# Attention values of a pair in two blocks, with a new chunk order, in a fused attention and expert kernel

## The chip, the cores and the metric

The kernel runs on one core of one Trainium2 chip. The metric is the device time of the whole kernel in microseconds. TensorE (PE; PEld is its weight load), VectorE (DVE), ScalarE (ACT), GpSimd (POOL) and SyncE (SP, the queue of plain DMAs) each run their own instructions in order and wait for one another by semaphores.

## The reference

```python
# attention: batch 8, heads 8, sequence 576, head size 64
scores = q @ k^T / 8
cum = cumsum(maximum(s, 0))
scores = where(j > i, -1e9, scores + minimum(cum[j] - cum[i], 0))
attn = exp(scores - max); attn = attn / (sum(attn) + 1e-9)
out = attn @ v                          # reshaped to x: 4608 rows of 512 (8 heads x 64)
# mixture of experts: 8 experts, 512 -> 1024 -> 512
logits = x @ w_gate + modality_bias[modality_id]
e = argmax(logits); gate = softmax(logits)[e]
y = gate * (relu(x @ w1[e]) @ w2[e])    # one expert a row
```

## The kernel before

The work has two stages. Attention runs over 32 pairs: a pair is one head in two batches (0 and 1 of `ab`), and eight pairs, one for each head, finish the rows of two batches. Then those rows are routed: their expert is chosen and they are scattered by expert into lists in DRAM. The expert stage (class `Moe`) reads the lists in blocks of 256 rows and streams the weights of the block's expert; its first weights are loaded during the last pairs.

**A pair.** The 576 query rows of each batch are cut into four chunks of 128 and a rest of 64; the two rests share one chunk. So a pair has nine chunks: 0 to 3 for batch 0, 4 to 7 for batch 1, and 8 for both rests. Chunk i (below 8) sees `128 * (i % 4 + 1)` keys, chunk 8 all 576. `ORDER` lists the chunks as they are worked. `run` (L334) has one step for each chunk of each pair, nine steps a pair, and each step issues in this order:

- `score` of the chunk. TensorE multiplies q and k in two matmuls (L236, L237; chunk 8 has eight, L250, L251): operands are split into a rounded high part and a low part. QH and KA hold high parts (KA's upper half k's low part), QL and KB the low part of q against the high part of k, and the bias rows. VectorE adds the mask and takes the extreme of each row (L239, L253), ScalarE takes the exponential and its row sum (L259). Four PSUM banks (`sp`) hold scores.
- in the steps named by `setup` and at fixed places: constants, and the loads of a later pair (`load`).
- one piece of `prep` of the next pair: POOL copies q and k to QH, KA and KB (`high`, L178) and subtracts for the low parts of k (L196, twice) and of q for batch 1 (L198). The low part of q for batch 0 (L192) is VectorE's, in the third piece. Each pair alternates between two sets of QH, QL, KA, KB.
- one piece of `tail` of the pair before.
- `trans` of the chunk that was scored three steps ago (`LAG`): TensorE transposes it in blocks of 128 into one of two PSUM banks (`pt`), and ScalarE (VectorE for chunk 8) copies it to PT (L272, L284). Chunk 8 takes two such banks, four blocks and one block. PT has three buffers for the batches of two pairs.
- one piece of routing, if a group of eight pairs is done (`Route.group`; L491 to L536: reductions and comparisons on VectorE, ten small matmuls, and nine scatters by POOL, one in four steps).

**The tail** starts when the last chunk in `ORDER` is transposed, and one step later (`TD`) issues the values: for both batches five matmuls over the keys into one bank `om` (queries 128 to 575, L307) and one into the bank `ox` (queries 0 to 127, L305). ScalarE copies the result to oT (L313, L314), VectorE the two rests (L317), side by side as a block diagonal. The next two steps multiply oT with pw, a matrix that is identity and w_gate side by side for each batch (L203), so that rows come out with their expert logits behind them (72 columns a row and head): first for chunks 0 and 1 of both batches, then for 2 and 3 and the rests, these in two matmuls of 72 columns that accumulate. VectorE scales the result by the reciprocal row sums (L311, L312) into x (L329, L331). These, the small matmuls of routing and oT's first part share the one bank `ox`.

**Order.** The program names which instruction an engine may take only after which (`issue_after`): the values come after all TensorE work issued ahead of them, and what is issued later stays behind them (`self.wall`). `self.hold[0]` is the newest mask and extreme on VectorE. Between these points a scheduler lays the instructions of each engine in an order of its own, guided by the order of issue.

Of the kernel before, what the change touches and what calls it, by code (L numbers as in the profile page):

```python
# [12 lines left out]
ALU = mybir.AluOpType  # L13
# [11 lines left out]
ORDER = (3, 7, 2, 1, 8, 6, 5, 0, 4)  # L25
# [6 lines left out]
class Attn:  # L32
# [3 lines left out]
    def __init__(self, ctx, tc, qkv, s, ident, consts):  # L36
# [15 lines left out]
        self.pw = c.tile([P, 8, 2 * XW], F32, name="pw")  # L52
        self.mk = c.tile([P, 800], F32, name="mk")
# [50 lines left out]
    def setup(self, wg):  # L104
        nc = self.nc
        wgv = wg.rearrange("(h d) e -> d h e", d=64)
        for ab in range(2):
            nc.sync.dma_start(self.pw[64 * ab:64 * ab + 64, :, XW * ab + 64:XW * ab + XW], wgv)

    def consts(self, t1):  # L110
# [29 lines left out]
        for ab in range(2):  # L140
            rows = slice(64 * ab, 64 * ab + 64)
            idv = self.ident[rows, 64 * ab:64 * ab + 64]
            nc.scalar.copy(self.pw[rows, :, XW * ab:XW * ab + 64], idv.unsqueeze(1).broadcast_to([64, 8, 64]))

# [23 lines left out]
    def prep(self, pi):  # L168
# [21 lines left out]
        for a in range(2):  # L190
            if a == 0:
                nc.vector.tensor_tensor(QL[lo, a, :KW], rq[lo, a], QHf[lo, a, :KW], ALU.subtract)  # L192
# [68 lines left out]
    def trans(self, st, i):  # L261
# [24 lines left out]
    def tail(self, st):  # L286
# [5 lines left out]
        o0 = self.ps2.tile([P, 512], F32, name="ox")  # L292
        om = self.ps2.tile([P, 448], F32, name="om")
# [3 lines left out]
        for j in (0, 1, 2, 3, 4, -1):  # L297
            q0 = max(P * j, P)
            for ab in range(2):
                r = slice(64 * ab, 64 * ab + 64)  # L300
                with ExitStack() as after:
                    for i in pe:
                        after.enter_context(self.tc.issue_after(i))
                    if j < 0:
                        m = nc.tensor.matmul(o0[r, :P], V[:, ab, 0, :], PT[ab][:, :P], start=True, stop=True)  # L305
                    else:
                        m = nc.tensor.matmul(om[r, q0 - P:], V[:, ab, j, :], PT[ab][:, PTS * j + q0 if j < 4 else PTW - 64:PTS * j + KW if j < 4 else PTW], start=j == 0, stop=j == 4)  # L307
                pe = [m.ins]
        self.wall = m.ins
        rs = self.sm.tile([P, 9], F32, name="rs")  # L310
        nc.vector.tensor_tensor(rs, st["sums"], self.eps, ALU.add)  # L311
        nc.vector.reciprocal(rs, rs)  # L312
        nc.scalar.copy(oT[:, :P], o0[:, :P])  # L313
        nc.scalar.copy(oT[:, P:512], om[:, :384])  # L314
        for ab in range(2):
            r = slice(64 * ab, 64 * ab + 64)
            nc.vector.tensor_copy(oT[r, 512 + 64 * ab:576 + 64 * ab], om[r, 384:])  # L317
        yield
        for g in range(2):
            xo = self.ps2.tile([P, 512], F32, name="ox")  # L320
            for u in range(2):
                c = 2 * g + u
                self.pw_(xo[:, 2 * XW * u:2 * XW * u + 2 * XW], oT[:, P * c:P * c + P], self.pw[:, h, :], start=True, stop=True)
            if g == 1:
                for ab in range(2):
                    self.pw_(xo[:, 4 * XW:5 * XW], oT[:, 512:], self.pw[:, h, XW * ab:XW * ab + XW], start=ab == 0, stop=ab == 1)
            src = xo[:, :4 * XW].rearrange("p (t d) -> p t d", t=4)
            rv = rs[:, 4 * g:4 * g + 4].unsqueeze(2).broadcast_to([P, 4, XW])
            nc.vector.tensor_tensor(x[g][:, :, :, h], src.rearrange("p t (d r) -> p t d r", r=2), rv.rearrange("p t (d r) -> p t d r", r=2), ALU.mult)  # L329
            if g == 1:  # L330
                nc.vector.tensor_scalar(x[2][:, 0, :, h], xo[:, 4 * XW:5 * XW].rearrange("p (d r) -> p d r", r=2), rs[:, 8:9], None, ALU.mult)  # L331
            yield

    def run(self, npair, newx, done, setup):  # L334
# [5 lines left out]
        prev, prepg, n = None, None, len(seq)  # L340
        for k in range(n + LAG + 9):
# [14 lines left out]
            nt = None  # L356
            if LAG <= k < n + LAG:
                p0, i0 = seq[k - LAG]
                if i0 == ORDER[-1]:
                    nt = sts[p0]  # L360
            if prev is not None:
                if next(prev, 0) == 0:
                    prev = None
                    if ps["pi"] % 8 == 7:
                        bg.append(done(ps["pi"] // 8, ps["x"]))
            if LAG <= k < n + LAG:
                with self.behind():
                    self.trans(sts[p0], i0)
            if nt is not None:
                prev, ps = self.tail(nt), nt  # L370
            if prev is None and k >= n + LAG:
                break
# [4 lines left out]
        assert prev is None  # L377
# [633 lines left out]
```

## Time and profile before

| what | us |
|---|---|
| three runs | 923.99, 926.44, 930.06 |
| median | 926.44 |
| profiled execution, its own time | 922.89 |
| its span, first to last instruction | 921.1 |
| first values block / last values block / first expert matmul group | 42.3 / 437.6 / 443.3 |

Of the span TensorE is busy 91%, VectorE 67%, POOL 63%, ScalarE 56%. The mean granted TensorE clock is 0.977 of full speed. A row in order of time has start, duration, engine, line, operation, tile written and tiles read, shapes, count, and in brackets the engine's idle time just before it with what ended it. Rows of groups have busy time, mean duration in ns, idle time and releaser. An f32 matmul shows as two records, and for the values the two batches run side by side in the two halves of the array's columns.

### The profile page before, as it was taken

Reading aid. Unit: us, or ns where it says so; the run is one execution under the profiler, and the core shown is the slowest. Engines: PE = TensorE matmul, PEld = TensorE weight load, DVE = VectorE, ACT = ScalarE, POOL = GpSimd, SP = SyncE. Lnnn points to the kernel's source line nnn. Section 1 sums busy time; section 2 is a strip of 40 time slices with the busy share of each in tenths; the row PEclk is TensorE's granted clock in tenths of the full one; section 3 lists DMA queues with packets and bytes.
Section 4 is the critical chain, followed back from the end, with each engine's and each line's share of the span. In section 5 each row is a group of like instructions: output and inputs, shape, how many; then the busy total and the mean of one; then the engine's idle time right before and its main releaser. Section 6 shows DMA issues by size and latency. Waiting matters only on the chain. (4 is left out here: it accounts for less than half of the span.)

```text
span 921.1 us, 16713 instructions
## 1 busy us (share of the span) xinstructions
PE 834.6 (91%) x5584; PEld 697.2 (76%) x5584; DVE 615.7 (67%) x1486; ACT 519.4 (56%) x1209; POOL 575.9 (63%) x478
## 2 busy tenths in 40 slices
PE   0799998999899898988879989999999999999984
PEld 0577776767677776755769879999999999999862
DVE  7487777657866587666657966666666556665681
ACT  3577776767677666757434445445444445444651
POOL 9676776887687876872266555555655556555760
PEclk9999999999999999989989989999999999999998
DMA  5654444454454545424758676666666666665940
GB/s 149 198 138 138 137 137 138 152 171 136 135 157 152 165 125 173 143 89 145 256 188 306 257 273 242 231 231 232 232 230 231 227 222 226 221 227 221 309 161 2
DMA packets 67562, 172.76 MB, mean 188 GB/s; under 512 B 12087, under 2 KB 12087, under 8 KB 67412
## 3 DMA queue, kind: packets, MB, share of 16 engines
q1 hardware_dynamic: 61620, 151.64, 48.8%
q0 software_dynamic: 5856, 20.06, 5.5%
q8 instruction: 44, 0.72, 0.3%
q14 instruction: 42, 0.34, 0.1%
HBM read 144.95 MB, written 26.80 MB: 186 GB/s over the span
## 5 line engine op out<-in xcount | busy, mean ns | idle before, releaser
L259 ACT ACTIVATE pe<-pe,mx 128x512 f32<-128x512 f32 (+3 forms) x256 | 144.1, 564 | 48.0 <-DVE mx L239 48.0
L272 ACT COPY PT<-pt 128x512 f32<-128x512 f32 (+3 forms) x256 | 106.5, 419 | 52.3 <-PE pt L269 49.5
L239 DVE CUSTOM_DVE_ANT_0 pe<-sp,mk 128x512 f32<-128x512 f32 (+3 forms) x256 | 117.3, 480 | 27.4 <-PE sp L237 24.0
L269 PE MATMUL pt<-ident,pe 128*128 128x128 f32 x640 | 119.2, 287 | 15.3 <-ACT PT L272 13.2
L825 ACT ACTIVATE hT<-hp 128x512 fp32r<-128x512 f32 x72 | 42.8, 595 | 158.7 <-PE hp L823 158.7
L809 POOL DMA_INDIRECT out<-ys,oi x36 | 39.9, 1110 | 141.7 <-DVE ys L808 55.7
L236 PE MATMUL sp<-KA,QH 128*128 128x256 f32 (+2 forms) x256 | 98.4, 392 | 20.1 <-DVE KA L196 16.0
L269 PEld LDWEIGHTS pt<-ident,pe 128*128 128x128 f32 x640 | 79.2, 146 | 42.5 <-ACT PT L272 29.8
L196 POOL TENSOR_TENSOR KA<-rawk,KA 64x576 fp32r<-64x576 f32 x63 | 93.8, 1506 | 20.3 <-DMA lists<-x,di 18.2
L237 PE MATMUL sp<-KB,QL 76*128 76x256 f32 (+2 forms) x256 | 85.2, 336 | 13.6 <-DMA QL<-oh 7.2
L823 PE MATMUL hp<-xT,wcb 128*128 128x256 f32 x648 | 90.1, 283 | 0.0
L307 PE MATMUL om<-PT,V 128*64 128x448 f32 (+3 forms) x640 | 89.6, 427 | 0.0
L826 DVE SCALAR_TENSOR_TENSOR hT<-hp,hT 128x512 fp32r<-128x512 f32 x72 | 49.2, 684 | 59.3 <-ACT hT L825 59.2
L823 PE MATMUL hp<-xT,wcc 128*128 128x256 f32 x528 | 77.4, 287 | 7.8 <-DVE hT L826 3.2
L823 PEld LDWEIGHTS hp<-xT,wcb 128*128 128x128 f32 x648 | 83.6, 189 | 0.6
L178 POOL TENSOR_SCALAR QH<-rawq 128x576 fp32r<-128x576 f32 x62 | 41.5, 671 | 64.0 <-issue 56.3
L802 PE MATMUL y<-wcb,hT 128*128 128x512 f32 x336 | 81.1, 398 | 0.0
L307 PEld LDWEIGHTS om<-PT,V 128*64 128x64 f32 x640 | 44.0, 139 | 46.8 <-issue 37.5
L823 PE MATMUL hp<-xT,wca 128*128 128x256 f32 x552 | 78.7, 285 | 0.4 <-ACT xT L788 0.3
L823 PEld LDWEIGHTS hp<-xT,wcc 128*128 128x128 f32 x528 | 70.8, 196 | 9.0 <-DVE hT L826 3.4
L802 PEld LDWEIGHTS y<-wcb,hT 128*128 128x128 f32 x336 | 62.8, 188 | 14.8
L823 PEld LDWEIGHTS hp<-xT,wca 128*128 128x128 f32 x552 | 72.3, 191 | 1.3 <-ACT xT L788 0.5
(270 smaller groups left out, 1946.7 us busy)
## 6 DMA issues: line engine op xcount, KB each, us to landing
wrbw<-in_w SPq DMA_DIRECT2D x104, 512.0 KB
wraw<-in_w SPq DMA_DIRECT2D x56, 512.0 KB
rawq<-in_qkv SPq DMA_DIRECT2D x32, 576.0 KB
rawk<-in_qkv SPq DMA_DIRECT2D x32, 576.0 KB
xg<-lists SPq DMA_DIRECT2D x18, 576.0 KB
V<-in_qkv SPq DMA_DIRECT2D x32, 320.0 KB
lists<-z SPq DMA_DIRECT2D x8, 576.0 KB
ekd<-ek SPq DMA_DIRECT2D x1, 1440.0 KB
```

The costliest lines, as they stand in the source:

```text
L196: self.last = (nc.vector if pi == 0 and a == 0 else nc.gpsimd).tensor_tensor(KA[up, a], rk[up, a], KAf[up, a], ALU.subtract).ins
L236: self.pe.append(nc.tensor.matmul(sp[:, :nn], QH[:, q0:q0 + P], KA[:, ab, :nn], start=True, stop=False).ins)
L237: self.pe.append(nc.tensor.matmul(sp[:, :nn], QL[:EXT, q0:q0 + P], KB[:EXT, ab, :nn], start=False, stop=True).ins)
L239: ins = nc.vector.tensor_tensor_reduce(out=t[:, :n], in0=sp[:, :n], in1=self.mk[:, 512 - n:512], scale=-0.125, scalar=3.0e38, op0=ALU.add, ...
L259: nc.scalar.activation(t[:, :n], t[:, :n], AF.Exp, bias=m, scale=-1.0, accum_out=st["sums"][:, o:o + 1])
L269: self.pe.append(nc.tensor.transpose(out=pt[:, P * j:P * j + P], in_=pe[:, P * j:P * j + P], identity=self.ident).ins)
L272: cp(w[:, :, v:v + P], pt[:, :P * (c + 1)].rearrange("p (j q) -> p j q", q=P))
L307: m = nc.tensor.matmul(om[r, q0 - P:], V[:, ab, j, :], PT[ab][:, PTS * j + q0 if j < 4 else PTW - 64:PTS * j + KW if j < 4 else PTW], star ...
L802: self.last[0] = nc.tensor.matmul(y[u], hT[:, a, f, P * u:P * u + P], W[4 + f // 2][:, c, 512 * (f % 2):512 * (f % 2) + 512], start=f == 0 ...
L823: nc.tensor.matmul(hp[:, u], W[k][:, a, f:f + P], xT[:, c, k], start=k == 0 and i == 0, stop=k == 3 and i == 2)
L825: nc.scalar.activation(hs, hp, AF.Relu)
L826: nc.vector.scalar_tensor_tensor(hT[:, 1, 2 * m:2 * m + 2], hp, 0.0, hs.bitcast(F32), ALU.max, ALU.subtract)
```

## The change

1. `ORDER` becomes 3, 7, 2, 6, 8, 1, 5, 0, 4: the chunks with the most keys first.
2. The tail is split in two. The large block (`g` = 1: queries 256 to 575, five matmuls for each batch) starts when chunk 8, fifth in the order, is transposed; the small one (`g` = 0: queries 0 to 255, two matmuls for each batch) when the last chunk is. Each has its own values, one copy to oT of 256 columns, one step with the packed matmuls, and its own reciprocal sums, placed behind the newest mask and extreme. So values of the large block come at the start of the next pair, those of the small one where all values stood before. Both use one bank `o`; `ox` is left to the packed matmuls and routing. Routing of a finished group starts one step earlier.
3. The fifth block of chunk 8's transpose goes to the free columns of the bank `o` instead of to a second `pt` bank.
4. The two packed matmuls of the rests become one, with a second matrix `pq` (identity and w_gate for both batches below each other), filled by two more copies and two more DMAs at the start. `s8` is made in place of `sr`.
5. The low part of q for batch 0 moves from the third piece of `prep` to the first, behind the newest mask and extreme.

```diff
-ORDER = (3, 7, 2, 1, 8, 6, 5, 0, 4)
+ORDER = (3, 7, 2, 6, 8, 1, 5, 0, 4)
...
+        self.pq = c.tile([P, 8, XW], F32, name="pq")
...
-            s8 = t1.tile([64, KW], F32, name="s8")
+            s8 = sr
...
+            nc.sync.dma_start(self.pq[64 * ab:64 * ab + 64, :, 64:], wgv)
...
+            nc.scalar.copy(self.pq[rows, :, :64], idv.unsqueeze(1).broadcast_to([64, 8, 64]))
...
+        with self.tc.issue_after(self.hold[0]) if self.hold[0] is not None else ExitStack():
+            nc.vector.tensor_tensor(QL[lo, 0, :KW], rq[lo, 0], QHf[lo, 0, :KW], ALU.subtract)
         yield
...
-            if a == 0:
-                nc.vector.tensor_tensor(QL[lo, a, :KW], rq[lo, a], QHf[lo, a, :KW], ALU.subtract)
...
-                pt = self.ps1.tile([P, 512], F32, name="pt")
+                if nj == 4:
+                    pt = self.ps1.tile([P, 512], F32, name="pt")
+                else:
+                    st["o"] = self.ps2.tile([P, 512], F32, name="o")
+                    pt = st["o"][:64, 384:]
...
-    def tail(self, st):
+    def tail(self, st, g):
...
+        q0, q1 = (256, KW) if g else (0, 256)
+        o = st["o"] if g else self.ps2.tile([P, 512], F32, name="o")
         oT = self.oT[st["pi"] % 2]
 
         pe, self.pe = self.pe, []
-        for j in (0, 1, 2, 3, 4, -1):
+        nj = 5 if g else 2
+        for j in range(nj):
+            f = max(P * j, q0)
...
+                    m = nc.tensor.matmul(o[r, f - q0:q1 - q0], V[:, ab, j, :], PT[ab][:, PTS * j + f if j < 4 else PTW - 64:PTS * j + q1 if j < 4 else PTW], start=j == 0, stop=j == nj - 1)
+            pe = [m.ins]
         self.wall = m.ins
...
+        nc.scalar.copy(oT[:, q0:q0 + 256], o[:, :256])
+        if g:
+            for ab in range(2):
+                r = slice(64 * ab, 64 * ab + 64)
+                nc.vector.tensor_copy(oT[r, 512 + 64 * ab:576 + 64 * ab], o[r, 256:320])
+        yield
+        n = 5 if g else 4
+        rs = self.sm.tile([P, 5], F32, name="rs")
+        with self.tc.issue_after(self.hold[0]):
+            nc.vector.tensor_tensor(rs[:, :n], st["sums"][:, 4 * g:4 * g + n], self.eps[:, :n], ALU.add)
+            nc.vector.reciprocal(rs[:, :n], rs[:, :n])
...
+        if g:
+            self.pw_(xo[:, 4 * XW:5 * XW], oT[:, 512:], self.pq[:, h, :], start=True, stop=True)
...
+                if i0 in (8, ORDER[-1]):
+                    g = int(i0 == 8)
+                    prev.append((self.tail(sts[p0], g), sts[p0], g))
```

More of the change, by code (lines that the diff above doesn't have):

```diff
@@ L311, in tail @@
[L311 to L317, printed above, removed]
-        yield
[L319 to L332, printed above, removed]
@@ new lines, in tail @@
+        n = 5 if g else 4
[3 more added lines that the diff above has]
+            nc.vector.reciprocal(rs[:, :n], rs[:, :n])
+        xo = self.ps2.tile([P, 512], F32, name="ox")
+        for u in range(2):
+            c = 2 * g + u
+            self.pw_(xo[:, 2 * XW * u:2 * XW * u + 2 * XW], oT[:, P * c:P * c + P], self.pw[:, h, :], start=True, stop=True)
@@ L355, in run @@
                     next(prepg, 0)
-            nt = None
+            if prev and next(prev[0][0], 0) == 0:
+                _, st, g = prev.pop(0)
+                if g == 0 and st["pi"] % 8 == 7:
+                    bg.append(done(st["pi"] // 8, st["x"]))
             if LAG <= k < n + LAG:
                 p0, i0 = seq[k - LAG]
[L359 to L366, printed above, removed]
                 with self.behind():
                     self.trans(sts[p0], i0)
-            if nt is not None:
-                prev, ps = self.tail(nt), nt
-            if prev is None and k >= n + LAG:
+                if i0 in (8, ORDER[-1]):
+                    g = int(i0 == 8)
+                    prev.append((self.tail(sts[p0], g), sts[p0], g))
+            if not prev and k >= n + LAG:
                 break
@@ L376, in run @@
                         bg.pop(0)
-        assert prev is None
+        assert not prev
         return bg
```

16 lines of the change are left out of this document (6 added, 10 removed).

## The prediction

> **What bounds the kernel now.** I read the page first, then the windows, then the order of time on TensorE, and only then the engines that release it.
>
> ```profile
> span 921.1 us, 16713 instructions
> ...
> PE 834.6 (91%) x5584; PEld 697.2 (76%) x5584; DVE 615.7 (67%) x1486; ACT 519.4 (56%) x1209; POOL 575.9 (63%) x478
> ...
> 500.00:921.00 421.00, 399.93 (x2517) 356.44 (x2515) 268.94 (x297) 194.03 (x242) 229.55 (x105) 0.98 0.60 219
> ```
>
> TensorE is busy 91% of the span. The last row (PE, PEld, DVE, ACT, POOL busy, granted clock, DMA share, GB/s) is the expert stage, which the diff does not touch: PE 399.93 of 421 us. So what attention gives up or wins should move the end by as much. Next, one pair in the attention stage, in order of time (start us, us, engine, line, tiles, count):
>
> ```profile
> 66.66 2.70 PE L307 MATMUL om<-PT,V 128*64 128x448 f32 x20
> ...
> 69.51 0.66 PE L269 MATMUL pt<-ident,pe 128*128 128x128 f32 x4
> ...
> 71.57 1.16 PE L203 MATMUL ox<-pw,oT 128*128 128x144 f32 x8
> ...
> 72.56 0.27 PE L269 MATMUL pt<-ident,pe 128*128 128x128 f32 x1
> ...
> 77.19 0.27 PE L269 MATMUL pt<-ident,pe 128*128 128x128 f32 x1
> 77.93 0.33 PE L269 MATMUL pt<-ident,pe 128*128 128x128 f32 x1 [0.46 <-ACT PT L272]
> ...
> 78.51 2.70 PE L307 MATMUL om<-PT,V 128*64 128x448 f32 x20
> ```
>
> From one values block (L307) to the next: 78.51 - 66.66 = 11.85 us, with a single wait in it, 0.46 us for ScalarE to empty a transpose bank. That is the undisturbed pair. Now the disturbed ones and the end:
>
> ```profile
> 137.50 2.70 PE L307 MATMUL om<-PT,V 128*64 128x448 f32 x20
> ...
> 143.70 0.76 PE L203 MATMUL ox<-pw,oT 128*128 128x144 f32 x4 [2.34 <-ACT oT L313]
> ...
> 153.37 2.70 PE L307 MATMUL om<-PT,V 128*64 128x448 f32 x20
> ...
> 188.95 2.70 PE L307 MATMUL om<-PT,V 128*64 128x448 f32 x20
> ...
> 198.67 0.50 PE L237 MATMUL sp<-KB,QL 76*128 76x512 f32 x1 [1.81 <-POOL QL L198]
> ...
> 203.74 2.70 PE L307 MATMUL om<-PT,V 128*64 128x448 f32 x20
> ```
>
> (a row of the windows, columns as in the expert stage's)
>
> ```profile
> 199.00:202.50 3.50, 3.50 (x19) 3.18 (x18) 2.98 (x10) 2.97 (x10) 3.50 (x6) 0.67 0.97 317
> ```
>
> (and the end, in order of time)
>
> ```profile
> 437.58 0.60 PE L307 MATMUL om<-PT,V 128*64 128x448 f32 x2
> ...
> 442.34 1.16 PE L203 MATMUL ox<-pw,oT 128*128 128x144 f32 x8 [0.55 <-DVE x L329]
> ...
> 443.33 1.04 PE L786 MATMUL tp<-ident,xg 128*128 128x128 f32 x8
> ```
>
> The interval after 137.50 is 15.87 us, 4.02 over the undisturbed; it holds the routing of the batch pair just finished, and recurs after the 16th and 24th pair. I call it the **routing pair**. The interval after 188.95 is 14.79 us, 2.94 over: 1.81 us of waiting for POOL's low part of q, then a granted clock of 0.67 in the next 3.5 us. It ends each stretch in which POOL scatters rows (three times); I call it the **scatter pair**. The expert stage starts at 443.33, directly behind the last packed matmuls. Three intervals before each scatter pair look undisturbed, but POOL falls behind in them. That leaves 14 intervals where only TensorE's own work and the 0.46 us count: eight before the first routing pair, and three in each of the two batches after it.
>
> **The change part by part.**
>
> *Fifth packed block.* One matmul for two: two of the eight records at 71.57 go. They take (72.56 - 71.57) / 8 = 0.124 us each, though two pairs of them have half the columns; so the weight loads set the pace, and a pair saves 0.25 us of TensorE.
>
> *Values in two blocks.* Columns for each head: 448 + 448 + 320 + 192 + 64 + 128 = 1600 before; 3 x 320 + 192 + 64 for the large block and 256 + 128 for the small one, 1600 again. Twelve matmuls a pair become fourteen, but the cost of a block is columns plus its ends. The rate, from two weight loads of 448-column matmuls (two heads at once):
>
> ```profile
> 204.17 0.14 PEld L307 LDWEIGHTS om<-PT,V 128*64 128x64 f32 x2 [0.23 <-issue]
> ...
> 204.54 0.14 PEld L307 LDWEIGHTS om<-PT,V 128*64 128x64 f32 x2 [0.23 <-issue]
> ```
>
> 0.37 us for 448 columns, twice per matmul: 1600 columns take 2.64 us, while 66.66 to 69.51 is 2.85. One end costs about 0.2 us, and a second block pays it again; between 0.1 and 0.35 (the gap in front of the block included) I take 0.25. So the packed saving is spent here: TensorE's work stays the same.
>
> *What the 0.46 us wait hangs on.* VectorE and ScalarE ahead of it:
>
> ```profile
> 73.56 1.01 DVE L284 COPY PT<-pt 128x256 f32<-128x256 f32 x4
> ...
> 76.40 1.16 DVE L192 TENSOR_TENSOR QL<-rawq,QH 64x576 fp32r<-64x576 f32 x1
> ...
> 78.21 0.65 DVE L311 TENSOR_TENSOR rs<-sums,eps 128x9 f32<-128x9 f32 x1
> ...
> 79.49 0.80 ACT L259 ACTIVATE pep<-pep,mx 128x576 f32<-128x576 f32 x1
> ...
> 73.11 0.67 POOL L178 TENSOR_SCALAR QH<-rawq 128x576 fp32r<-128x576 f32 x1 [3.36 <-issue]
> ...
> 77.04 3.17 POOL L196 TENSOR_TENSOR KA<-rawk,KA 64x576 fp32r<-64x576 f32 x2
> ```
>
> Before the values, three large chunks are scored in a row while TensorE has only small transposes; ScalarE's exponentials queue up, and L192 (1.16 us) holds VectorE among their reductions. Then the 2.85 us values block lets both go idle. With the large block after the first score of the next pair, some 2 us of TensorE work lie between the scores of chunks 3 and 7, and L192 now sits there: POOL starts QH at 73.11 and ends its first half at 73.78, ahead of the reduction of chunk 3, so L192 does not wait for POOL in an undisturbed pair. The 0.46 us should go. Without that cover it would cost VectorE its 1.16 us again.
>
> *What is late next.* (1) The large block needs the four copies of chunk 8 (1.01 us of VectorE, at 73.56), which were five steps early before. Between its transposes and the block now stand the scores of chunks 4 and 3 and two transposes; 77.19 - 72.56 = 4.63 us hold six scores and ten transposes, so these are about 1 us: no margin, 0 to 0.3 us. (2) The packed matmuls of the small block need ScalarE's copy, which queues behind the 0.80 us exponential of chunk 8; before, 2.85 us of values lay over it, now the small block, 384 columns x 2 x 0.37 / 448 = 0.63 us and its ends, about 0.9. Wait 0 to 0.5. I take 0.1 for both together, since TensorE can fill either with scores that are ready. Net for an undisturbed pair: 0.46 - 0.1 = 0.36 us, and 14 x 0.36 = **5 us**. ScalarE's copies to oT stay level (512 columns in two copies, before and after). (3) The sums for the reciprocal now go in two parts; the large block's add stands in the step behind that block, where VectorE has little room and POOL is in L196. The row at 78.21 is this add beside L196 as it is now, 0.65 us; I keep that row, which the reductions behind it can bear.
>
> The Trainium skill, page "SBUF — State Buffer", section "SBUF: two separate sides", says that a VectorE instruction with two SBUF inputs and a GpSimd instruction that reads SBUF take one shared port pair as an exclusive lock, and the loser waits out the other's whole instruction. By it the add could be held for a whole L196 instead of 0.65 us, and the sum below would be that of the second rival, a loss.
>
> *Scatter pairs and the three before each.* POOL sets the pace there:
>
> ```profile
> 193.02 2.79 POOL L196 TENSOR_TENSOR KA<-rawk,KA 64x576 fp32r<-64x576 f32 x2 [2.31 <-DMA lists<-x,di]
> ...
> 197.22 1.39 POOL L198 TENSOR_TENSOR QL<-rawq,QH 64x576 fp32r<-64x576 f32 x1
> ```
>
> A faster TensorE only waits longer for L198. Scatters start one step earlier, same number. **0 us**, between -2 and +2 for each of three; L192 ahead of a late POOL can hold VectorE, up to about 1 us, mostly under the large block.
>
> *Routing pairs.*
>
> ```profile
> 136.29 3.31 POOL L196 TENSOR_TENSOR KA<-rawk,KA 64x576 fp32r<-64x576 f32 x2
> ...
> 138.26 1.43 DVE L496 TENSOR_TENSOR lg<-lg,rmx 128x72 f32<-128x72 f32 x1
> ...
> 139.96 1.22 DVE L500 SCALAR_TENSOR_TENSOR oh<-lg,ew 128x72 f32<-128x72 f32 x1
> ...
> 142.14 0.23 DVE L503 TENSOR_TENSOR ohb<-oh,rmx 128x72 bf16<-128x72 f32 x1
> ...
> 74.49 0.27 DVE L239 CUSTOM_DVE_ANT_0 pe<-sp,mk 128x128 f32<-128x128 f32 x1
> ...
> 74.70 0.68 DVE L239 CUSTOM_DVE_ANT_0 pe<-sp,mk 128x512 f32<-128x512 f32 x1
> ```
>
> L503, of the same size, takes 0.23; L496 ends with POOL's L196 (138.26 + 1.43 = 139.69, 136.29 + 3.31 = 139.60). The lost 1.2 and 1.0 us make VectorE late, ScalarE with it, and TensorE waits 2.34. In the new order routing starts one step earlier (the small block ends sooner), so VectorE's list after POOL's first QH is the copies of chunk 8 (1.01), the reductions of chunks 4 and 3 (0.27 + 0.68), L192 (1.16) and two small routing operations (0.23 each): L496 starts about 3.6 us after that QH, and L196 comes 3.9 us after it (73.11 to 77.04). L496 slips out, L500, a step later, probably stays under. One of two: 1.5 us of the 4.02, between 0 and 3.3. 3 x 1.5 = **4.5 us**.
>
> *Ends.* From 437.58 to 443.33 lie 5.75 us of values, copies and two packed groups in line; after the change only the small block, a copy and two packed matmuls remain, roughly 3 us. I take **2.5 us**, between 0 and 3.5. At the start:
>
> ```profile
> 14.79 1.25 ACT L143 COPY pw<-ident 64x512 f32<-64x512 f32 x2
> ...
> 30.33 0.72 ACT L259 ACTIVATE pe<-pe,mx 128x512 f32<-128x512 f32 x1 [13.08 <-DVE mx L239]
> ...
> 28.38 1.44 SPq L108 DMA_DIRECT2D pw<-in_wg  x2
> ```
>
> Two more copies for pq (1.25 us) fit in ScalarE's 13.08 idle us. Two more DMAs hold SP's queue 1.44 us ahead of the loads of the third pair: 0 to 1.4 us once, taken as 0.3. In-place s8 costs nothing.
>
> Sum: 5 + 0 + 4.5 + 2.5 - 0.3 = 11.7, say **12 us**. The profiled execution ran 922.89 us with its span of 921.1; it would go to 911. The median of the runs shown is 926.44, so I predict **914 us**. About 1% (9 us) is what a measurement can tell from no change.
>
> **The rivals.**
> - *The wait comes back* (0.25): the copies of chunk 8 or the small block's copy cost as much as the 0.46 us, and routing stays under L196. For it: the two margins above. Against: the large block gives VectorE and ScalarE time in every pair. Only the end is won: 924.
> - *The port* (0.13, slower): the add for the reciprocal (L311) moves to the step after the large block, where POOL runs L196 and VectorE has oT copies, reductions of 7, 2, 6 and 8 and the scaling in one stretch. Held as L496 was, it costs up to 1.43 where it shows 0.65 now; the 2.85 us cover is gone, and the packed matmuls of the small block wait. Price 0.8 us more than now less 0.36, near 0.5 in 28 pairs: +14, 940. It decides once the hold exceeds the 0.36 us won.
> - *All of it* (0.12): no new waits, at 0.55 a pair (8), routing pairs free (10), the end (2.5), scatter pairs shorter as L196 loses no time to VectorE (5): 901.
> - *The forecast* (0.50): 906 to 920.
>
> The lock rule of the Trainium skill (same page and section) is the mechanism of the second rival; the trace agrees with it at 139.6, where L496 ends within 0.1 us of L196.
>
> **How the numbers follow.** Range 900 to 929: it holds the forecast, the first and third rival with their spread, and leaves out the second and a few per cent. Faster by over 1% (below 917): 0.42 of the forecast plus 0.12 = 0.54. Within 1%: 0.08 + 0.25 = 0.33. Slower: 0.13.
>
> **What would show it.** The distance from large block to large block should be near 11.5; L192 right after chunk 3's reduction; no wait of transposes for ScalarE ahead of values; L496 near 0.25, the wait of 2.34 shorter; six records, not eight, in the packed group; less than 4 us from the last values to the expert stage. I am wrong if TensorE waits on each of the two packed groups, if the scheduler put L192 or the sums elsewhere, or if the expert stage starts earlier but waits for weights.

## The result and the profile after

The changed kernel took 910.95 us (median of 906.14 to 913.58) beside 925.22 us for the kernel before on the same chip: a ratio of 0.984, 95% interval 0.980 to 0.988. Five rounds on another chip, at the end of the study, gave 0.990 (0.987 to 0.994). The profiled execution ran 906.14 us.

Page of the kernel after:

```profile
span 904.4 us, 16875 instructions
...
PE 824.9 (91%) x5648; PEld 714.2 (79%) x5648; DVE 635.5 (70%) x1550; ACT 523.7 (58%) x1211; POOL 579.4 (64%) x478
```

The row of its windows for the expert stage (columns as before: PE, PEld, DVE, ACT, POOL, granted clock, DMA share, GB/s):

```profile
500.00:904.40 404.40, 383.87 (x2406) 340.27 (x2405) 254.62 (x256) 188.20 (x236) 223.04 (x101) 0.98 0.60 220
```

The shares are nearly as before, the span is shorter. One undisturbed pair in order of time on TensorE:

```profile
81.45 0.87 PE L312 MATMUL o<-PT,V 128*64 128x256 f32 x8
82.25 0.66 PE L272 MATMUL pt<-ident,pe 128*128 128x128 f32 x4
...
86.31 2.37 PE L312 MATMUL o<-PT,V 128*64 128x320 f32 x20
88.61 0.44 PE L272 MATMUL pt<-ident,pe 128*128 128x128 f32 x2
...
89.35 0.66 PE L206 MATMUL ox<-pw,oT 128*128 128x144 f32 x4
89.84 0.34 PE L206 MATMUL ox<-pq,oT 128*128 128x72 f32 x2
90.02 0.27 PE L272 MATMUL pt<-ident,pe 128*128 128x128 f32 x1
...
92.57 0.87 PE L312 MATMUL o<-PT,V 128*64 128x256 f32 x8
```

From small block to small block 92.57 - 81.45 = 11.12 us instead of 11.85, and no row of this pair has a wait in brackets. The two blocks take 0.80 (81.45 to 82.25) and 2.30 us (86.31 to 88.61), 3.10 for 2.85 before; the packed group of the large block has six records, not eight, and with the small block's four the packed work falls from 1.49 to 1.16 us (sums of the starts of these rows and the next ones).

A routing pair, a scatter pair, and the last scatter pair, in order of time on several engines (POOL's durations are rough):

```profile
133.74 2.77 POOL L199 TENSOR_TENSOR KA<-rawk,KA 64x576 fp32r<-64x576 f32 x2
...
134.03 1.19 DVE L497 TENSOR_TENSOR lg<-lg,rmx 128x72 f32<-128x72 f32 x1
...
135.65 0.44 PE L206 MATMUL ox<-pq,oT 128*128 128x72 f32 x2 [1.20 <-DVE oT L319]
...
136.45 0.22 DVE L501 SCALAR_TENSOR_TENSOR oh<-lg,ew 128x72 f32<-128x72 f32 x1
...
136.59 1.43 POOL L201 TENSOR_TENSOR QL<-rawq,QH 64x576 fp32r<-64x576 f32 x1
...
170.06 1.84 DVE L190 TENSOR_TENSOR QL<-rawq,QH 64x576 fp32r<-64x576 f32 x1 [1.77 <-POOL QH L181]
...
391.73 0.18 DVE L595 CAST ftf<-fti 128x18 f32<-128x18 int32 x1 [1.59 <-POOL fti L593]
...
392.42 0.68 DVE L242 CUSTOM_DVE_ANT_0 pe<-sp,mk 128x512 f32<-128x512 f32 x1
...
394.27 0.76 PE L206 MATMUL ox<-pw,oT 128*128 128x144 f32 x4 [2.09 <-ACT oT L315]
...
396.50 1.31 DVE L577 TENSOR_TENSOR foh<-foh,fa 128x48 f32<-128x48 f32 x1
397.83 0.23 DVE L319 COPY oT<-o 64x64 f32<-64x64 f32 x1
...
398.12 0.70 PE L206 MATMUL ox<-pq,oT 128*128 128x72 f32 x2 [2.99 <-DVE oT L319]
...
403.11 0.91 PE L312 MATMUL o<-PT,V 128*64 128x256 f32 x8
```

and two windows behind its waits:

```profile
398.00:403.00 5.00, 4.88 (x19) 4.52 (x19) 4.94 (x20) 1.82 (x5) 2.52 (x2) 0.50 0.00 0
411.00:417.00 6.00, 5.79 (x24) 4.78 (x25) 0.93 (x4) 2.69 (x7) 2.35 (x1) 0.51 0.43 162
```

VectorE's list now holds L497 under POOL's L199, as L496 was held before, but L501 takes 0.22 us at the change from L199 (ends 136.51) to L201. In the scatter pairs TensorE no longer waits for POOL's QL; VectorE waits, ahead of its own subtraction, for POOL's late QH (1.77 us at 170.06), and TensorE for the copies that VectorE makes behind it (L319: 13.7 us in 12 waits over the kernel). The last scatter pair is the one that got worse. VectorE sits idle 1.59 us for POOL's L593, a step of the counting behind the last scatters, and the reduction at 392.42 stands behind it; later L577, counting too, takes 1.31 us between the two copies of L319. TensorE waits 2.09 and 2.99 us, then its granted clock is 0.50, and 0.51 once more in the pair behind it. The low clock as such is not new: in the kernel before it was 0.50 in 200.21 to 203.62, 302.61 to 306.02, 405.01 to 411.84 and 425.49 to 428.90, 17.1 us of attention, and in the kernel after in 396.41 to 403.23 and 410.06 to 416.89, 13.7 us.

Where the span went, by the starts of the values blocks (L307 before, the small block of L312 after; # counts pairs, so #4-8 is from the fourth block to the eighth):

| stretch | before | after | difference |
|---|---|---|---|
| start to #1 (the large block now lies ahead of the mark) | 42.32 | 44.51 | +2.2 |
| first three intervals (#1-4) | 36.19 | 36.94 | +0.8 |
| eight undisturbed intervals (#4-8, #14-16, #22-24) | 94.83 | 89.34 | -5.5 |
| routing, three times two intervals (#8-10, #16-18, #24-26) | 82.34 | 72.74 | -9.6 |
| scatters of groups 1 and 2 (#10-14, #18-22) | 101.74 | 101.79 | 0.0 |
| last scatters (#26-30) | 51.51 | 57.80 | +6.3 |
| #30-32 | 28.65 | 26.29 | -2.4 |
| #32 to the first expert matmuls | 5.75 | 2.35 | -3.4 |
| expert stage | 477.8 | 472.7 | -5.1 |

Attention gives 11.6 of the 16.7 us between the two profiled executions. The rest is in a stage that the diff doesn't touch; it measured 472.7 to 478.8 us over all profiles of this study, why is not shown, and it is left out of what follows. A difference of a few us between two medians can therefore lie in that stage. Attention itself varies too: in after_again, a second profile of the same kernel, the first three intervals take 35.45 us and the first expert matmuls come 2.5 us later.

### The profile page after: what moved, and what is told of

It is laid out like the page before. It is cut to its first block, busy times and chain, and to the rows that moved or that the text cites. A ratio compares the mean times of both kernels' runs of the same rounds, so it can differ in the third digit from the quotient of the medians.

```text
span 904.4 us, 16875 instructions
## 1 busy us (share of the span) xinstructions
PE 824.9 (91%) x5648; PEld 714.2 (79%) x5648; DVE 635.5 (70%) x1550; ACT 523.7 (58%) x1211; POOL 579.4 (64%) x478
## 5 line engine op out<-in xcount | busy, mean ns | idle before, releaser
L242 DVE CUSTOM_DVE_ANT_0 pe<-sp,mk 128x512 f32<-128x512 f32 (+3 forms) x256 | 119.8, 485 | 30.6 <-PE sp L240 28.1
L275 ACT COPY PT<-pt 128x512 f32<-128x512 f32 (+3 forms) x256 | 104.5, 421 | 50.2 <-PE pt L272 46.9
L239 PE MATMUL sp<-KA,QH 128*128 128x256 f32 (+2 forms) x256 | 104.5, 412 | 20.0 <-DVE KA L199 16.7
L312 PE MATMUL o<-PT,V 128*64 128x320 f32 (+4 forms) x896 | 108.5, 369 | 4.3 <-DVE PT L291 4.2
L312 PEld LDWEIGHTS o<-PT,V 128*64 128x64 f32 x896 | 77.9, 138 | 40.1 <-DVE PT L291 16.4
L199 POOL TENSOR_TENSOR KA<-rawk,KA 64x576 fp32r<-64x576 f32 x63 | 88.6, 1424 | 25.9 <-DMA lists<-x,di 17.5
L824 PE MATMUL hp<-xT,wcb 128*128 128x256 f32 x648 | 89.8, 282 | 0.0
L272 PEld LDWEIGHTS pt<-ident,pe 128*128 128x128 f32 x640 | 77.2, 145 | 12.6 <-issue 5.3
L824 PE MATMUL hp<-xT,wcc 128*128 128x256 f32 x528 | 74.3, 280 | 7.3 <-DVE hT L827 4.6
L824 PEld LDWEIGHTS hp<-xT,wcc 128*128 128x128 f32 x528 | 67.8, 188 | 8.6 <-DVE hT L827 5.0
```

Of the source, the lines that this page charges most:

```text
L199: self.last = (nc.vector if pi == 0 and a == 0 else nc.gpsimd).tensor_tensor(KA[up, a], rk[up, a], KAf[up, a], ALU.subtract).ins
L239: self.pe.append(nc.tensor.matmul(sp[:, :nn], QH[:, q0:q0 + P], KA[:, ab, :nn], start=True, stop=False).ins)
L242: ins = nc.vector.tensor_tensor_reduce(out=t[:, :n], in0=sp[:, :n], in1=self.mk[:, 512 - n:512], scale=-0.125, scalar=3.0e38, op0=ALU.add, ...
L272: self.pe.append(nc.tensor.transpose(out=pt[:, P * j:P * j + P], in_=pe[:, P * j:P * j + P], identity=self.ident).ins)
L275: cp(w[:, :, v:v + P], pt[:, :P * (c + 1)].rearrange("p (j q) -> p j q", q=P))
L312: m = nc.tensor.matmul(o[r, f - q0:q1 - q0], V[:, ab, j, :], PT[ab][:, PTS * j + f if j < 4 else PTW - 64:PTS * j + q1 if j < 4 else PTW], ...
```

## The experiments

Each run is a ratio to the kernel before on the same chip; "pair" is an interval between #4 and #8, "eight" the sum of the eight undisturbed intervals of the table above, "first expert" the start of the first expert matmuls.

| run | median us | ratio (95%) | pair us | eight us | first expert us |
|---|---|---|---|---|---|
| before | 922.4 to 926.4 | 1 | 11.85 | 94.8 | 443.3 |
| after | 910.95 | 0.984 (0.980-0.988) | 11.12 | 89.3 | 431.7 |
| after_again | 913.47 | 0.990 (0.987-0.994) | 11.1 | 89.3 | 434.2 |
| only_q_low_moved | 922.62 | 1.000 (0.997-1.002) | 11.69 | 93.5 | 443.7 |
| order_only | 936.85 | 1.017 (1.011-1.022) | 12.3 | 98.6 | 459.3 |
| order_and_q_low | 915.28 | 0.991 (0.989-0.994) | 11.33 | 90.7 | 435.3 |
| q_low_back | 936.48 | 1.013 (1.011-1.016) | 12.48 | 99.9 | 459.7 |
| q_low_back_held | 917.09 | 0.994 (0.992-0.997) | 12.1 to 12.2 | 96.4 | 438.0 |
| fifth_in_pt | 925.51 | 1.003 (1.000-1.005) | 12.48 | 96.1 | 447.8 |
| old_order | 909.17 | 0.986 (0.983-0.988) | 11.3 to 11.5 | 94.9 | 430.6 |
| two_packed | 933.67 | 1.011 (1.007-1.015) | 11.6 to 12.0 | 94.2 | 453.5 |
| rests_by_scalar | 912.68 | 0.988 (0.986-0.991) | 11.11 | 90.6 | 438.0 |
| spread | 905.91 | 0.984 (0.979-0.989) | 11.11 | 89.8 | 426.2 |
| spread_first | 899.18 | 0.974 (0.971-0.976) | 11.12 | 89.7 | 426.8 |

One limit holds for all: the scheduler lays an engine's instructions anew after each edit. In spread it moved POOL's alone and in q_low_back chiefly VectorE's; in most others all engines differ, so a run prices the edit together with the order that came of it. The undisturbed pairs of one run can differ too: where "eight" is well off eight times "pair", the later ones have another order.

### What took the wait away: the first two edits on the kernel before

only_q_low_moved, the kernel before with the low part of q in the first piece:

```diff
+        with self.tc.issue_after(self.hold[0]) if self.hold[0] is not None else ExitStack():
+            nc.vector.tensor_tensor(QL[lo, 0, :KW], rq[lo, 0], QHf[lo, 0, :KW], ALU.subtract)
         yield
...
-            if a == 0:
-                nc.vector.tensor_tensor(QL[lo, a, :KW], rq[lo, a], QHf[lo, a, :KW], ALU.subtract)
```

> The kernel before, with only the low part of q moved to the first piece of prep. Theory (split and move work together): without the block of values at that place VectorE has no idle time there, so the interval goes from 11.85 to about 11.7 and the time to 921 to 924. Rival (the move alone brings most of it): the 0.46 us wait goes, pairs take 11.3 us, time 912 to 915.

No difference in time. The eight undisturbed intervals win 1.3 us and the three routing stretches 4.4 (77.9 for 82.3), and the scatter stretches of groups 1 and 2 (105.0 for 101.7) and #26-32 (82.5 for 80.2) give it back. The wait for ScalarE's copy is smaller, not gone (order of time on TensorE):

```profile
101.14 0.82 PE L269 MATMUL pt<-ident,pe 128*128 128x128 f32 x5 [0.24 <-ACT PT L272]
```

order_only, the kernel before with the new order alone:

```diff
-ORDER = (3, 7, 2, 1, 8, 6, 5, 0, 4)
+ORDER = (3, 7, 2, 6, 8, 1, 5, 0, 4)
```

> The kernel before with the new order of the chunks alone (3, 7, 2, 6, 8, 1, 5, 0, 4): one values step of both blocks, q's low part as before. Theory (the gain needs the split, the early subtraction and the order together): the order alone lets nothing go earlier, since the values still wait for chunk 4's copies; 922 to 930, a pair of 11.7 to 12.2 us. Rival (large chunks first spread the copies so that TensorE no longer waits for a pt bank, and that is where most of the gain is): a pair of 11.3 us and 912 to 916.

Slower than the theory or the rival had it, 1.7%. VectorE and TensorE in one pair, and then the row of the waits over the whole kernel (total us, times, longest):

```profile
110.13 1.20 DVE L192 TENSOR_TENSOR QL<-rawq,QH 64x576 fp32r<-64x576 f32 x1 [0.30 <-POOL QH L178]
111.26 1.00 DVE L284 COPY PT<-pt 128x256 f32<-128x256 f32 x4
...
112.14 0.67 PE L269 MATMUL pt<-ident,pe 128*128 128x128 f32 x4 [0.58 <-DVE PT L284]
```

```profile
PE pt L269 <- DVE PT L284: 22.7, 25, 3.0
```

In this order q's low part stands on VectorE ahead of the four copies of chunk 8, and TensorE waits for the bank that they empty.

order_and_q_low, both edits, the values still in one step:

> The kernel before with two edits together, the new order of the chunks and q's low part in the first piece with its hold; one values step of both blocks. Theory (the order alone cost 13 us because VectorE's queue then had the subtraction, 1.20 us, ahead of the copies of chunk 8, which TensorE waited for; with the subtraction moved that is gone): the 21.2 us of waits on L284's tiles fall below 6, an undisturbed pair takes 11.5 to 11.7 us instead of 12.33, and the time is 915 to 923. Rival (the order itself brings chunk 8's two transposed banks too close to the next ones, wherever the subtraction stands): the pair stays above 12.1 us and the time is 930 to 938.

```profile
100.31 2.70 PE L307 MATMUL om<-PT,V 128*64 128x448 f32 x20
...
111.64 2.70 PE L307 MATMUL om<-PT,V 128*64 128x448 f32 x20
...
118.53 1.01 DVE L284 COPY PT<-pt 128x256 f32<-128x256 f32 x4
...
120.28 0.98 DVE L187 TENSOR_TENSOR QL<-rawq,QH 64x576 fp32r<-64x576 f32 x1
```

The subtraction now follows the copies; the pair falls to 11.33 us, below what the theory said, and TensorE has no wait in it. The time is the theory's, and beside after_again on the same chip the two ratios can't be told apart (0.991 and 0.990). So two of the change's five edits, one of no effect and one that costs 1.7% alone, bring the whole kernel's time to within what these runs resolve of the full change. The split, the bank and the single packed matmul add 0.21 us a pair to that (1.4 us over the eight).

### What the split needs: edits taken back from the kernel after

q_low_back, the subtraction back in the third piece, as in the kernel before:

```diff
-        with self.tc.issue_after(self.hold[0]) if self.hold[0] is not None else ExitStack():
-            nc.vector.tensor_tensor(QL[lo, 0, :KW], rq[lo, 0], QHf[lo, 0, :KW], ALU.subtract)
...
+            if a == 0:
+                nc.vector.tensor_tensor(QL[lo, a, :KW], rq[lo, a], QHf[lo, a, :KW], ALU.subtract)
```

> The changed kernel, with the low part of q back in the third piece of prep. Theory (split and move work together: the move frees VectorE where it is full, the large block covers it): an undisturbed pair takes 11.4 to 11.6 us instead of 11.12, TensorE waits for ScalarE or VectorE again in each pair, and the time is 916 to 920; in pairs where POOL is late VectorE no longer waits for QH (1.77 us at 170). Rival (the split alone carries it): pairs stay at 11.1 and the time at 911 or a little below.

1.3% slower than the kernel before, some 25 us from after. VectorE in one pair, and the waits of the whole kernel:

```profile
111.25 1.20 DVE L195 TENSOR_TENSOR QL<-rawq,QH 64x576 fp32r<-64x576 f32 x1
112.38 0.74 DVE L291 COPY PT<-pt 128x256 f32<-128x256 f32 x2
```

```profile
PE o L312 <- DVE PT L291: 35.6, 26, 5.5
```

The same row as in order_only: 1.20 us of subtraction ahead of chunk 8's copies, and this time it is the large block that waits.

q_low_back_held puts the same two lines in the third piece too, but inside the hold on the newest reduction:

```diff
...
+            if a == 0:
+                with self.tc.issue_after(self.hold[0]) if self.hold[0] is not None else ExitStack():
+                    nc.vector.tensor_tensor(QL[lo, a, :KW], rq[lo, a], QHf[lo, a, :KW], ALU.subtract)
```

> The kernel after, with the low part of q back in the third piece of the preparation as in the run before this one (936.5), but told to be placed after the group's reduction. Theory (what cost there was the place VectorE's queue gave the instruction, ahead of the copies of chunk 8, so that the values waited 25 times for L291): the copies stand ahead of it again, the waits of the values for the copies on L291 fall from 34.8 us to under 8, an undisturbed pair takes 11.1 to 11.6 us instead of 12.5, and the time is 912 to 920. Rival (the piece counts: by the third piece the subtraction is too late for the pair that needs it, or POOL is the one delayed, wherever it stands on VectorE): score matmuls wait for QL or VectorE's copies stay late, the pair stays above 12.2 us, and the time is 930 to 938.

The time is the theory's (917), the pair is neither's: some 12.15 us.

```profile
106.66 0.74 DVE L196 TENSOR_TENSOR QL<-rawq,QH 64x576 fp32r<-64x576 f32 x1
...
111.80 0.42 DVE L292 COPY PT<-pt 128x256 f32<-128x256 f32 x1 [0.33 <-PE pt L286]
```

The subtraction is no longer in front of the copies (they now wait for TensorE), and the 35.6 us of waits became 6.0, in two waits. With them most of the loss goes (the ratio falls from 1.013 to 0.994), which points to the place in VectorE's list. TensorE still spends 1.0 us more in a pair than in after, some 0.46 of it waiting for ScalarE's oT copy; every engine has another order here, so what the piece itself costs stays open.

fifth_in_pt gives the fifth block of chunk 8 a transpose bank again:

```diff
-                if nj == 4:
-                    pt = self.ps1.tile([P, 512], F32, name="pt")
-                else:
-                    st["o"] = self.ps2.tile([P, 512], F32, name="o")
-                    pt = st["o"][:64, 384:]
+                pt = self.ps1.tile([P, 512], F32, name="pt")
...
-        o = st["o"] if g else self.ps2.tile([P, 512], F32, name="o")
+        o = self.ps2.tile([P, 512], F32, name="o")
```

> The kernel after, with the fifth packed block of chunk 8 back in a bank of its own among the transposes' banks, and the accumulator allocated where the values begin. Theory (TensorE ran short of transposed banks once or twice a pair, which is what the 0.6 us between the pairs' starts was in the kernel before): the waits of pt for PT come back, 0.2 to 0.5 us of idle in an undisturbed pair of 11.12, so 11.3 to 11.6 us and, over the 14 undisturbed intervals, 3 to 7 us: 914 to 919. Rival (the split's order and the shorter values blocks alone took the wait away, the bank is worth nothing): the pair stays at 11.1 us and the time at 909 to 913.

The whole gain is gone. Waits of TensorE within one of the pairs of 12.48 us, within one of the four later undisturbed pairs (#14-16, #22-24), which take 11.55 us, and over the whole kernel:

```profile
120.49 0.76 PE L206 MATMUL ox<-pw,oT 128*128 128x144 f32 x4 [0.58 <-ACT oT L311]
...
124.20 0.41 PE L272 MATMUL pt<-ident,pe 128*128 128x128 f32 x2 [0.35 <-DVE PT L287]
...
206.96 0.87 PE L308 MATMUL o<-PT,V 128*64 128x256 f32 x8
...
212.00 0.41 PE L272 MATMUL pt<-ident,pe 128*128 128x128 f32 x2 [0.36 <-DVE PT L287]
...
218.51 0.87 PE L308 MATMUL o<-PT,V 128*64 128x256 f32 x8
```

```profile
PE pt L272 <- DVE PT L287: 18.3, 28, 5.0
```

The later pairs are the theory: one wait of 0.36 us for the bank, and 0.43 us more than the 11.12 of after. The early ones grew by 1.36 us, of which two waits make 0.93; the larger one is not for a bank but for a late oT copy, which came with the new order of the engines. Of the 14 to 16 us by which attention is longer than in the two profiles of after, the eight intervals hold 6.7; the bank's own share is not priced beyond the 0.36 us a pair.

old_order keeps the split with the old `ORDER`, the large block after chunk 6:

```diff
-ORDER = (3, 7, 2, 6, 8, 1, 5, 0, 4)
+ORDER = (3, 7, 2, 1, 8, 6, 5, 0, 4)
...
-                if i0 in (8, ORDER[-1]):
-                    g = int(i0 == 8)
+                if i0 in (6, ORDER[-1]):
+                    g = int(i0 == 6)
```

> The kernel after with the old order of the chunks (3, 7, 2, 1, 8, 6, 5, 0, 4): the large block follows chunk 6, the sixth of nine, instead of chunk 8, the fifth; split, early subtraction and the bank stay. Theory (the order is what makes the split free: with it each block's products and copies lie four and five steps apart): the blocks stand three and six steps apart, some copies come late again, an undisturbed pair takes 11.2 to 11.6 us, 912 to 919. Rival (the order only serves to end the large chunks first, one step matters nothing): 11.12 us and 909 to 912. Second rival (chunk 6's copies are then the last that the large block waits for, 0.3 to 0.6 us in every pair): 919 to 928.

As fast as after, though an early pair is 0.2 us longer: the pair is the theory's, the time the first rival's. The intervals #14-16 and #22-24 take 12.0 to 13.1 us, so that the eight need 94.9 us, no less than in the kernel before; the time is won elsewhere, most of it in the last pairs (#26-32 take 78.4 us, 84.1 in after). With the early subtraction, then, either the new order (915) or the split in the old one (909) is enough for the time, but the eight undisturbed intervals in sum are shorter only with the new order.

two_packed (two accumulating matmuls for the rests again) and rests_by_scalar (the rests copied by ScalarE):

```diff
-            self.pw_(xo[:, 4 * XW:5 * XW], oT[:, 512:], self.pq[:, h, :], start=True, stop=True)
+            for ab in range(2):
+                self.pw_(xo[:, 4 * XW:5 * XW], oT[:, 512:], self.pw[:, h, XW * ab:XW * ab + XW], start=ab == 0, stop=ab == 1)
```

> The changed kernel, with the packed matmul of the rests as two that accumulate again (pq filled but not used). Theory (weight loads set the pace, 0.124 us a record): two records more, an undisturbed pair 11.12 + 0.25 = 11.37 us; over some 20 pairs in which TensorE is the bound the time rises by 4 to 6 us, to about 916. Rival (it is hidden behind other waits): 911, pairs at 11.12.

```diff
-                nc.vector.tensor_copy(oT[r, 512 + 64 * ab:576 + 64 * ab], o[r, 256:320])
+                nc.scalar.copy(oT[r, 512 + 64 * ab:576 + 64 * ab], o[r, 256:320])
```

> The changed kernel, with the two copies of the rests to oT done by ScalarE instead of VectorE. Theory (in routing and scatter pairs VectorE is held by POOL's port or by the wait for QH, and only these copies pass it on to TensorE): the waits of TensorE for them, 13.7 us in 12 places, go, and the time falls to 900 to 905; undisturbed pairs stay at 11.12. Rival (VectorE is late in all it does, so the next reduction or scaling makes TensorE wait as long): 909 to 912, the wait moves to L242 or L334.

In two_packed the best pair (#14-15) is 11.36 us, 0.25 over after, as much as the matmul was worked out to cost; the other 20 us of the run came with other orders of all engines (waits for L319 alone are 17.9 us, 13.7 in after), so it doesn't price the edit. rests_by_scalar took the waits for L319 away, and others grew in their place (POOL's KA from 3.2 to 7.9 us, POOL's QL from none to 3.6, ScalarE's oT copies from 5.9 to 7.0): no gain.

### The disturbed pairs

after_again is the unchanged kernel, for the chip of the last four runs.

> The kernel after, unchanged, as the yardstick for the three that share its chip. Every theory: a ratio to before of 0.980 to 0.988, some 908 to 913 us, and an undisturbed pair of 11.12 us.

spread issues the scatters of the first two groups every six steps; only POOL's list changes:

```diff
-            for _ in range(SCS):
+            for _ in range(6 if bp < 2 else SCS):
```

> The kernel after, with the scatters of the first two groups issued every 6 steps instead of every 4, so that POOL's preparation has more room beside them. Theory (in the scatter pairs VectorE's subtraction waits for a QH that POOL makes late, 1.77 us on L190, and TensorE then 1.20 us for the copies on L319 behind it; the stretch is POOL's): these waits go, the intervals of the scatter pairs fall from about 11.9 to 11.2-11.5 us, 8 such intervals, 2 to 5 us: 906 to 909. Rival (the scatters only move into pairs that had been free, where POOL has as little room): the same waits in other pairs, 909 to 913, no difference from after.

By the profile the stretches #10-16 and #18-24 fall from 73.04 and 73.62 to 69.89 and 69.92 us, 6.9 together, VectorE's waits for QH at L190 go from 16.0 us (11 times) to 6.8 (5 times), and the first expert matmuls come 5.5 us earlier; by the times of the runs the ratio is the same as after's, with intervals as wide as that gain. Alone it isn't settled.

spread_first adds a second edit to that: the counting behind the third group's scatters (`first`) in five pieces instead of two, its three index vectors made at the start (that part is not shown).

```diff
...
         n = self.count("f", self.cnt, 256)
+        yield
         inc, exc, bf, oh, pick = self.spread("f", n, 8, N2)
         yield
-        ex, s = pick(self.e, "ex"), pick(exc, "s")
+        ex = pick(self.e, "ex")
+        yield
+        s = pick(exc, "s")
+        yield
```

> The kernel after with two things done in its disturbed pairs: the scatters of the first two groups every 6 steps instead of 4, and the counting that follows the third group's scatters cut into six pieces instead of two, its three index vectors made once at the start. Theory (the last scatter pair took 20.5 us because VectorE's queue had that counting, waiting for POOL, ahead of the copies of the rests on L319): the pair takes 12.5 to 15 us, 5 to 8 us less; with 1 to 5 us of the spread scatters 899 to 905. Rival (the counting is only put into the pairs behind, which end later by as much, since POOL is full there): 905 to 910.

0.974 (0.971 to 0.976) beside after_again's 0.990: faster than both kernels, by 14 us than after_again. The last scatter pairs in order of time on TensorE, and the window behind them:

```profile
383.09 0.87 PE L312 MATMUL o<-PT,V 128*64 128x256 f32 x8
...
396.67 0.44 PE L206 MATMUL ox<-pq,oT 128*128 128x72 f32 x2 [3.19 <-DVE oT L319]
...
401.04 0.87 PE L312 MATMUL o<-PT,V 128*64 128x256 f32 x8
...
412.90 0.87 PE L312 MATMUL o<-PT,V 128*64 128x256 f32 x8
```

```profile
401.00:413.00 12.00, 11.80 (x90) 9.70 (x91) 8.80 (x42) 9.46 (x26) 2.59 (x2) 1.00 0.45 133
```

The pair itself missed its 12.5 to 15 us: 17.95, still with one wait of 3.19 for L319. The larger part is the next one, 11.86 us at full clock, where after had 17.17 (403.11 to 420.28) with the second stretch at 0.51. The two pairs together: 29.8 instead of 37.7. The third behind them takes 11.51 instead of 9.12, as the rival had it, so 4.96 us of #26-32 remain (79.13 for 84.09). The spread scatters give little in this run: #10-16 and #18-24 take 72.89 and 73.25 us, near after's 73.04 and 73.62, and the first expert matmuls come no earlier than in spread. They come 7.5 us earlier than in after_again; where the rest of the 14 us of the medians lies is not shown, as the profile of spread_first is of its slowest execution (903.2 us) and that of after_again of its fastest (908.6).

## Why the prediction was right, and where its steps were not

The forecast was 914 us, measured were 910.95, and attention gave 11.6 us of the predicted 12. That the sum comes out so close is in part luck: its terms were off in both directions.

- **Undisturbed pairs**, predicted 5 us, 0.36 in each of 14 intervals: 5.5 in eight of them, 0.69 each. The first three lost 0.8, and in the other three (#8-9, #16-17, #24-25, booked under routing) the kernel before took 11.58 us and had no such wait to lose. The wait was taken from its row, 0.46; by the starts of the neighbouring rows (77.19 to 77.93, where 0.14 is their usual distance) it was 0.60. The 0.1 for new waits was not spent, and the packed records gave 0.33, not 0.25. The second block cost 0.25, as worked out.
- **What the wait hung on.** The step named both the large block's place and L192's. Shown: the subtraction moved plus the new order remove it without any split (11.33 us). That L192 would cost its 1.16 us again without cover fits q_low_back, where the pair grew by 1.36 us; in order_only it grew by 0.5.
- **The bank of the fifth block** was given no term at all. That step failed: the wait for it is 0.36 us a pair, and with the order that the scheduler makes without it the pair grows by 0.43 to 1.36 us and the whole gain is gone.
- **Routing pairs**, predicted 1.5 each: 9.6 in all, less three undisturbed shares of 0.7 leaves 2.5 each, within the 0 to 3.3. The step had L496 slip out and L500 stay; it went the other way round. The wait of 2.34 became 1.20, and all waits of TensorE in these two intervals (#8-10) fell from 3.20 to 1.36 us. The subtraction alone brings 4.4 of the 9.6 (only_q_low_moved, 77.9 for 82.3), with the new order it is 5.5 (order_and_q_low, 76.9); the rest came with the whole change and is not taken apart.
- **Scatter pairs**, predicted 0 within 2 each: right for two, wrong for the third, +6.3. There the counting stands on VectorE between the reductions and L319; the prediction priced POOL's lateness and not what else of VectorE's list lay there. With the counting cut up (spread_first) #26-32 falls from 84.1 to 79.1 us, the kernel before took 80.2; but old_order takes 78.4 there with the counting whole, so the order of the engines counts as well. The 2.4 us won in #30-32 stand in no term of the prediction.
- **Ends**, predicted 2.5 less 0.3: 3.4 from the last block to the expert stage, less the 2.2 by which the first mark comes later, leaves 1.2. The step took what no longer follows the last mark as won, and did not count that the first large block (2.30 us) now lies ahead of the first mark.
- **The rivals.** "The wait comes back" fell: no wait in the pair. Without the early subtraction it would have been the outcome, and worse. "The port": the large block's add (L324) had a mean of 0.50 us in five undisturbed pairs (79 to 124 us), not 1.43, and no packed matmul waits for it; in the scatter pairs it took 1.5 to 1.9 us (at 184.7, 282.8 and 380.4), so the hold is there, but not in the 28 pairs of the rival.

## What to carry to other kernels

When a scheduler orders the engines, look first at which instruction stands ahead of the copies that the busiest engine waits for: here one 1.2 us subtraction made the same order of chunks worth +1.7% or -0.9%. Edits of such a change are not a sum; take each back alone before believing in any of them, and price what frees a bank as carefully as what saves an instruction. Then look at the few disturbed intervals: in the last of them, #26-32, runs of nearly the same kernel differ by 5 us and more, as much as the change won in eight undisturbed pairs together.

## What the runs showed of the hardware

Two things were not expected. First, VectorE's subtraction of 64 x 576 took 0.74 us where POOL was idle (q_low_back_held, at 242.38), 1.20 in q_low_back beside two of POOL's copies (111.25), and 3.10 in spread beside a train of POOL's copies:

```profile
191.04 3.10 DVE L190 TENSOR_TENSOR QL<-rawq,QH 64x576 fp32r<-64x576 f32 x1 [0.39 <-POOL QH L181]
...
191.61 1.30 POOL L181 TENSOR_SCALAR KA<-rawk 128x576 fp32r<-128x576 f32 x2
192.88 1.79 POOL L181 TENSOR_SCALAR KB<-rawk 64x576 fp32r<-64x576 f32 x2
```

It lasted through several POOL instructions, not one, and it ended at 194.14, 0.60 us after the first of the two KB copies (193.54); those two took 1.79 us, while the two KA copies ahead of them took 1.30. The Trainium skill, page "SBUF — State Buffer", section "SBUF: two separate sides", gives the shared port to whichever instruction starts first, for the whole of it, and blocks the other; it does not say how long the loser waits when several follow each other, and here that was four. That the port is the cause is inferred from these times.

Second, TensorE's granted clock fell to 0.50 over 396.41 to 403.23 after waits of 2.09 and 2.99 us with 0.86 us of matmuls between them (394.27 to 395.13). In the kernel before, a single wait of 1.81 us (to 198.67) was followed by 0.50 from 200.21 on. In the traces of this case the changes of the granted clock lie whole multiples of some 3.41 us apart (in the kernel before 200.21, 203.62 and 302.61: one step and 29). Two such steps for each of the two falls, as rows of windows, after and then before:

```profile
392.99:396.41 3.42, 0.87 (x5) 0.62 (x5) 3.42 (x13) 1.61 (x5) 3.34 (x7) 1.00 0.00 0
396.41:399.82 3.41, 1.70 (x6) 1.61 (x7) 3.35 (x8) 0.02 (x1) 3.33 (x3) 0.50 0.00 0
```

```profile
196.80:200.21 3.41, 1.60 (x11) 1.16 (x10) 1.58 (x7) 0.68 (x2) 3.34 (x5) 1.00 1.03 282
200.21:203.62 3.41, 3.41 (x16) 3.23 (x15) 3.31 (x11) 3.20 (x12) 3.33 (x5) 0.50 0.71 260
```

In the attention stage of these two kernels each of the six falls follows a step in which TensorE was busy for 0.87 to 1.86 us of the 3.41, so for about half of it or less. The limit is not sharp: the step from 241.17 of the kernel before, busy for 1.71 us, was not followed by a fall. The Trainium skill, page "TensorE: Matmul & The Clock Gate", section "HAM oscillation — how this bites in real kernels", asks for no idle gap above some 3.4 us; here shorter ones were enough.
